# Loading v as rows behind the turn, 64x64 tap tiles and a reordered front in a convolution-plus-MLP kernel

## The chip, the cores and the metric

The kernel runs on one core of one Trainium2 chip. The metric is the device time of one execution in microseconds. The profile names the engines PE (TensorE matmul), PEld (TensorE weight load), DVE (VectorE), ACT (ScalarE), POOL (GpSimd) and SP (SyncE, which issues most DMAs).

## The reference

One sequence of 2048 tokens with 512 channels, all inputs bf16:

```python
x = A_q
# block A, on q = layernorm(x)
k_shift[t] = sum_j k[t - j] * shift_k[:, j]            # 4 taps, each channel by itself
kv = k_shift * v
y  = causal_convolution(kv, ssm_k) + kv * ssm_D        # length 2048, each channel; fft in the reference
h  = x + layernorm(x) * y
# block B
h2 = h + relu(layernorm(h) @ w1) @ w2                  # w1 512x1376, w2 1376x512
```

## The kernel before, in words

The long convolution is computed with a two-stage transform of length 4096 made of matrix products. A token is written as 64a + t, with a from 0 to 31 and t from 0 to 63. Every engine works through its own instructions in the order in which the program issues them (`manual_schedule`): the lists of calls in the code are the schedule.

**Start.** `load_rows` (L96) loads ssm_k as rows into `kfl`: partition 32 rg + a, then t, a half d and 64 channels, in runs of 128 bytes. Two of the four quarters `rg` are issued on SP, two on ACT. SP then issues four pairs of DMA transposes, a chunk of 512 tokens of k into `kT` and of v into `vT` (channels on partitions), then the first 512 tokens of x (`x0`), then w1. POOL, DVE and ACT meanwhile make the tables: index patterns by iota, angles by `_turns` (DVE), sines by `_sin` (ACT): `f1hi` and `f1lo` for the first stage, `tab` for the second. `negated` (POOL, L224) writes the negative copies of `tab`. `wdiag` holds the tap weights as diagonal 128x128 matrices.

**Front.** Eight first-stage blocks of ssm_k (`stage1`, L297), 64 small products each in four tiles of 32 rows, with ssm_D added as a spike at time zero; two evictions per block into `a1k`, one on ACT and one on DVE. Eight `taps` (L335): four diagonal products for each of two channel groups of a 512-token chunk, whose eviction on DVE multiplies by v in place (L342). Sixteen `second_k` (L360): the second stage of ssm_k, in place in `a1k`. Four `row` calls (`to_rows`, L285) turn the product k*v, as pairs of bf16 in 32-bit words, into the row layout `xfl`. Between them stand the statistics and the normalisation of the first 512 tokens (`stats`, `norm_rows`), the column means of w1 (PE, ACT) and its centring (POOL, L378).

**Pairs.** `stage1_pairs` (L320): the first stage of the row data, eight blocks, evicted into `a1x`.

**Product.** For each of 16 `kp`, `product` (L484) makes the second stage of `a1x` in two orders (`u2`, `u1`) and multiplies both by `a1k`: one on DVE, the other on DVE too or, for ten of the sixteen, through a copy on ACT (`usb`) on POOL (L498). `last_table` writes the tables of the inverse's last stage.

**After it** come the inverse transform, the gate with x and its norm, the two MLP products with ReLU on ACT, and the output, in an order written out by hand.

PSUM is eight banks as four tiles of two banks, handed out in turn from two pools (`bank2`, L278). SBUF pools are opened and closed as the work proceeds, and a new pool takes the bytes of a closed one: its first writer waits for the last readers of what lay there.

Of the kernel before, what the change touches and what calls it, by code (L numbers as in the profile page):

```python
# [15 lines left out]
P = 128  # L16
# [39 lines left out]
def kernel(  # L56
# [37 lines left out]
    kfl = front.tile([P, 64, 2, 64], BF16, name="kfl")  # L94

    def load_rows(eng, rg):  # L96
        for d in range(2):
            src = bass.AP(tensor=A_ssm_k.tensor, offset=A_ssm_k.offset + S * (P * rg + 64 * d), ap=[[64, 32], [S, 64], [1, 64]])
            eng.dma_start(out=kfl[32 * rg:32 * rg + 32, :, d, :], in_=src)

    wsh = consts.tile([P, DC, KS], BF16, name="wsh")
    nc.scalar.dma_start(out=wsh[:], in_=A_shift_k.rearrange("(r p) j -> p r j", p=P))
    scratch = rows.tile([P, 4096], I32, tag="r", name="scratch")
    drow = scratch[:, 4064:4096].bitcast(BF16)
    nc.gpsimd.memset(drow, 0.0)
    nc.scalar.dma_start(out=drow[0:P:16, :], in_=A_ssm_D.rearrange("(r g) -> r g", g=64))
    load_rows(nc.scalar, 1)
    for rg in (0, 2):
        load_rows(nc.sync, rg)
    vT = front.tile([P, DC, S], BF16, name="vT")  # L110
    CH = 512
    kT = [front.tile([P, DC, CH + 16], BF16, name=f"kT{c}") for c in range(4)]
    nc.vector.memset(kT[0][:, :, 0:16], 0.0)
    for c in range(4):
        if c == 0:
            nc.sync.dma_start_transpose(out=kT[c][:, :, 16:CH + 16], in_=k_d[0:CH, :])
        else:
            nc.sync.dma_start_transpose(out=kT[c][:], in_=k_d[CH * c - 16:CH * c + CH, :])
        nc.sync.dma_start_transpose(out=vT[:, :, CH * c:CH * c + CH], in_=v_d[CH * c:CH * c + CH, :])

    x0 = front.tile([P, 4, D], BF16, name="x0")
    for b, src in enumerate(_tokens(x_d, 0, 4)):
        nc.sync.dma_start(out=x0[32 * b:32 * b + 32].rearrange("p t d -> p (t d)"), in_=src)


    w1 = w1p.tile([P, DC, DFF], BF16, name="w1")
    for i in range(2):
        for d in range(2):
            nc.sync.dma_start(out=w1[64 * i:64 * i + 64, 2 * d:2 * d + 2],
                                in_=B_w1.rearrange("(c i d g) f -> i d g c f", c=2, i=2, d=2)[i, d])  # L130
# [31 lines left out]
    r2 = scratch[:, 0:1024].rearrange("p (a b) -> p a b", b=64)  # L162
    nc.gpsimd.iota(r2, pattern=[[2, 16], [128, 64]], base=1, channel_multiplier=0)
    ident = consts.tile([P, P], BF16, name="ident")
# [8 lines left out]

    ind = consts.tile([P, P], BF16, name="ind")
    nc.gpsimd.memset(ind[:], 0.0)
    for s in range(0, P, 32):
        nc.gpsimd.affine_select(out=ind[s:s + 32, :], in_=ind[s:s + 32, :], compare_op=ALU.not_equal, fill=1.0,
                                base=0, pattern=[[-1, P]], channel_multiplier=4)

# [11 lines left out]
    load_rows(nc.scalar, 3)  # L191
# [11 lines left out]
    nc.gpsimd.memset(f1w[:], 0.0)  # L203
    for rg in range(DC):
        for i, f in enumerate((f1hi, f1lo)):
            nc.gpsimd.tensor_copy(out=f1w[32 * rg:32 * rg + 32, i, rg % 2, :], in_=f[32 * rg:32 * rg + 32, :])
    wdiag = rows.tile([P, DC, KS, P], BF16, name="wdiag")
    for rg in range(DC):
        nc.gpsimd.tensor_tensor(out=wdiag[:, rg, :, :], in0=ident[:].unsqueeze(1).to_broadcast([P, KS, P]),
                                in1=wsh[:, rg, :].unsqueeze(2).to_broadcast([P, KS, P]), op=ALU.mult)  # L210
    wm = rows.tile([P, 4, 344], F32, name="wm")
    ones = consts.tile([P, P], BF16, name="ones")
    nc.gpsimd.memset(ones[:], 1.0 / D)

    def turns2(i, b):
        ta = scratch[:, 1024 * (b + 1):1024 * (b + 2)].rearrange("p (a b) -> p a b", b=64)
        _turns(ta, r2, n2c[:], 8192, o2[:, i, b:b + 1])
        return ta
# [7 lines left out]

    o2 = consts.tile([P, 2, 2], F32, name="o2")
    for i in range(2):
        for b in range(2):
            nc.vector.tensor_scalar(out=o2[:, i, b:b + 1], in0=n2c[:], scalar1=32.0 * i, scalar2=4096.0 + 2048.0 * b,  # L230
                                    op0=ALU.mult, op1=ALU.add)
    for b in range(2):
        sines2(0, b, turns2(0, b))
    negated(0)
    negated(1)
# [12 lines left out]
    nc.gpsimd.iota(r3[:], pattern=[[1, 64]], base=0, channel_multiplier=0)  # L248
    for i, (top, bottom) in enumerate(((64.0, 96.0), (48.0, 80.0), (32.0, 64.0), (6144.0, 8192.0))):
        nc.gpsimd.memset(ow[0:64, i:i + 1], top)  # L250
        nc.gpsimd.memset(ow[64:128, i:i + 1], bottom)
    for i in range(3):
        nc.gpsimd.tensor_scalar(out=t3[:, i, :], in0=r3[:], scalar1=n2c[:], scalar2=ow[:, i:i + 1], op0=ALU.mult, op1=ALU.add)
    nc.gpsimd.memset(hsc[:], 0.0)
    nc.gpsimd.memset(hbi[:], 0.0)
    nc.gpsimd.tensor_scalar(out=k1o[:], in0=k1c[:], scalar1=2.0, scalar2=1.0, op0=ALU.mult, op1=ALU.add)
    for b in range(4):
        q = slice(32 * b, 32 * b + 32)
        nc.gpsimd.memset(hsc[q, b % 2:b % 2 + 1], TURN / 8192)
        nc.gpsimd.memset(hbi[q, b % 2:b % 2 + 1], -0.5 * TURN)  # L260
        nc.gpsimd.tensor_scalar(out=ofc[q], in0=k1o[q], scalar1=32.0 * (b % 2), scalar2=ow[q, 3:4], op0=ALU.mult, op1=ALU.add)
    nc.gpsimd.iota(rf[:], pattern=[[1, NT], [16, 2], [64, 32]], base=0, channel_multiplier=0)
    nc.gpsimd.tensor_scalar(out=rf[:], in0=rf[:], scalar1=k1o[:], scalar2=ofc[:], op0=ALU.mult, op1=ALU.add)
# [21 lines left out]
    def to_rows(src, q, fl):  # L285
        words = src[:].bitcast(F32).rearrange("p c (a b) -> p c a b", b=32)
        pst = bank2("pst")
        for i in range(8):
            nc.tensor.transpose(out=pst[:, i // 4, P * (i % 4):P * (i % 4) + P], in_=words[:, :, :, 8 * q + i], identity=identw[:])
        nc.vector.tensor_single_scalar(out=fl[:].bitcast(I32)[:, :, :, 8 * q:8 * q + 8],  # L290
                                       in_=pst[:].bitcast(I32).rearrange("p b (i d g) -> p g d (b i)", i=4, d=2),
                                       scalar=0, op=ALU.bitwise_or)
# [4 lines left out]
    def stage1(fl, a_out, gb, engs, spike=False):  # L297
# [9 lines left out]
        for gi in range(8):  # L307
            for f, first in ((f1hi, True), (f1lo, False)):
                for rg in range(4):
                    rw = slice(32 * rg, 32 * rg + 32)  # L310
                    nc.tensor.matmul(out=outs[rg][:, gi, :], lhsT=fl[rw, 8 * gb + gi, :, :].rearrange("p d n -> p (d n)"),  # L311
# [23 lines left out]
    def taps(c, h):  # L335
        ps = bank2("pkv")
        for i in range(2):
            for j in range(KS):
                nc.tensor.matmul(out=ps[:, i, :], lhsT=wdiag[:, 2 * h + i, j, :],  # L339
# [58 lines left out]
    def stats(src, mv, r, q):  # L398
        for i in range(4):
            nc.vector.bn_stats(out=st[:, i, :], in_=src[:, i, :])  # L400
# [359 lines left out]
```

## Time and profile before

| | us |
|---|---|
| median of 3 runs | 211.91 (211.48 to 212.68) |
| the profiled execution | 212.53 |
| its span, first to last instruction | 210.8 |
| granted TensorE clock, mean | 0.984 |
| PE busy | 176.0 (84%) |
| DVE busy | 146.5 (69%) |
| ACT busy | 93.6 (44%) |
| POOL busy | 91.5 (43%) |

The profile is one execution, with times from its span's start. A line of a group reads: source line, engine, operation, output<-inputs, shapes, count | busy us, mean ns of one | idle us just before, and what ended that idle time. A line of the timeline begins with its start and its length in us. A line of stretches gives, after the stretch and its length, the busy time (and number of instructions) of PE, PEld, DVE, ACT and POOL, the granted clock, the DMA share and GB/s.

### The profile page before, as it was taken

The numbers are of one execution on the slowest core, as the hardware profiler recorded it, in microseconds if no ns is written. First come the engines' busy times: TensorE is split into PE (matmuls) and PEld (weight loads), VectorE is DVE, ScalarE is ACT, GpSimd is POOL, SyncE is SP. The second block draws the span as 40 slices with busy tenths as digits, with TensorE's granted clock in tenths as the row PEclk, the third lists the DMA queues.
The fourth block names the chain that finished last, engine by engine and source line by source line (L and its number), as shares of the span: only waits on it lengthen the run. The fifth ranks groups of instructions, "written<-read, shape, count | busy, mean of one in ns | idle before, by whom it ended". The sixth has DMA issues, their size and how long they took to land.

```text
span 210.8 us, 4349 instructions
## 1 busy us (share of the span) xinstructions
PE 176.0 (84%) x1787; PEld 107.3 (51%) x1787; DVE 146.5 (69%) x236; ACT 93.6 (44%) x108; POOL 91.5 (43%) x109
## 2 busy tenths in 40 slices
PE   0329696998989587777796899999999999999993
PEld 0125343557768475665665564545455444444452
DVE  2615988459968689999998987988988381343042
ACT  0333535456288756651399447700560056016400
POOL 4899855402069569999298452031040002002000
PEclk9999997999999999999997999999999999999999
DMA  8999999920000000000780261251250215121012
GB/s 124 217 257 177 161 151 225 218 59 2 3 0 3 3 0 5 0 3 0 193 205 3 50 215 53 50 51 28 69 106 0 60 45 99 25 50 25 3 45 55
DMA packets 47315, 16.00 MB, mean 76 GB/s; under 512 B 42720, under 2 KB 46144, under 8 KB 47296
## 3 DMA queue, kind: packets, MB, share of 16 engines
q1 hardware_dynamic: 38400, 14.61, 35.5%
q10 hardware_dynamic: 8896, 1.12, 3.4%
q8 instruction: 14, 0.23, 0.5%
q14 instruction: 5, 0.04, 0.1%
HBM read 7.54 MB, written 2.10 MB: 46 GB/s over the span
## 4 chain that ended last, share of the span: by engine, by line
PE 59%; DVE 24%; ACT 4%; issue 4%; DMA 3%; ACTq 2%; POOL 1%; DVEq 0%; POOLq 0%
PE m L630 18%; PE m L684 17%; PE pkv L339 7%; DVE a1x L493 6%; DVE zs L523 5%; PE u L352 4%; DMA kfl<-in_A_ssm_k_dram 3%; DVE a1k L498 3%; PE pz L550 3%; PE ps L326 3%; PE ps2k L352 3%; DVE xfl L290 2%; ACT a1x L273 2%; PE pz L560 2%; DVE vT L342 2%
## 5 line engine op out<-in xcount | busy, mean ns | idle before, releaser
L666 ACT ACTIVATE h1T<-m 128x512 bf16<-128x512 f32 (+1 forms) x44 | 25.9, 597 | 43.6 <-PE m L630 43.6
L630 PE MATMUL m<-hT,w 128*128 128x512 bf16 (+1 forms) x176 | 39.0, 379 | 0.2 <-ACT hT L597 0.2
L684 PE MATMUL m<-w,h1T 128*128 128x512 bf16 (+1 forms) x165 | 36.3, 379 | 0.0
L690 DVE SCALAR_TENSOR_TENSOR o<-m,rstd,hp 128x256 bf16<-128x256 f32 x32 | 13.8, 478 | 27.6 <-PE m L684 26.6
L404 POOL TENSOR_SCALAR rstd<-mv 128x4 f32<-128x4 f32 x8 | 1.8, 228 | 71.2 <-DVE mv L402 71.2
L630 PEld LDWEIGHTS <-w 128*128 128x128 bf16 (+1 forms) x176 | 17.4, 100 | 20.4 <-issue 0.8
L498 POOL TENSOR_TENSOR a1k<-usb,a1k 128x1024 fp32r<-128x1024 f32 x10 | 23.7, 2396 | 5.3 <-DVE a1x L493 5.2
L684 PEld LDWEIGHTS <-h1T 128*128 128x128 bf16 (+1 forms) x165 | 15.9, 98 | 19.4 <-issue 0.3
L352 PE MATMUL u<-a1x,tab 64*128 64x256 f32 x256 | 19.8, 292 | 6.5 <-DVE a1x L493 2.4
L531 ACT CAST a1x<-zs 128x1024 fp32r<-128x1024 f32 (+2 forms) x10 | 17.2, 1717 | 11.9 <-DVE zs L523 11.9
L352 PEld LDWEIGHTS u<-a1x,tab 64*128 64x128 f32 x256 | 16.4, 185 | 9.8 <-issue 4.9
L493 DVE TENSOR_TENSOR a1x<-u,a1k 128x1024 fp32r<-128x1024 f32 x16 | 19.1, 1217 | 2.4 <-PE u L352 2.4
L529 POOL CAST a1x<-zs 128x1024 fp32r<-128x1024 f32 (+1 forms) x8 | 15.6, 1955 | 8.3 <-DVE zs L523 8.3
L523 DVE STREAM_TRANSPOSE zs<-pi 128x1024 f32<-128x1024 f32 x16 | 18.4, 1213 | 0.5 <-PE pi L518 0.5
L339 PE MATMUL pkv<-kT,wdiag 128*128 128x512 bf16 x64 | 18.5, 441 | 0.2 <-ACT a1k L273 0.2
L518 PE MATMUL pi<-a1k,wd 128*128 128x512 f32 x32 | 13.9, 434 | 2.9 <-DVE a1k L496 1.1
L342 DVE TENSOR_TENSOR vT<-pkv,vT 128x1024 bf16<-128x1024 f32 x8 | 9.8, 1221 | 9.2 <-PE pkv L339 8.2
L273 ACT CAST a1k<-ps2k 128x1024 fp32r<-128x1024 f32 x12 | 11.7, 1013 | 8.8 <-PE ps2k L352 8.8
L492 ACT COPY usb<-u 128x1024 f32<-128x1024 f32 x10 | 10.1, 1017 | 10.6 <-POOL a1k L498 8.7
L518 PE MATMUL pi<-a1x,wd 128*128 128x512 f32 x32 | 13.1, 408 | 0.0
L275 DVE CAST a1k<-ps 128x1024 fp32r<-128x1024 f32 x8 | 9.6, 1215 | 5.0 <-PE ps L311 5.0
L224 POOL TENSOR_SCALAR tab<-tab 128x1024 fp32r<-128x1024 f32 x4 | 11.0, 2775 | 4.4 <-ACT tab L146 4.3
(104 smaller groups left out, 268.3 us busy)
## 6 DMA issues: line engine op xcount, KB each, us to landing
xall<-in_A_q_dram SPq DMA_DIRECT2D x16, 128.0 KB, 3.3
out_dram<-o SPq DMA_DIRECT2D x62, 32.0 KB, 1.6
w<-in_B_w_dram SPq DMA_DIRECT2D x4, 344.0 KB, 7.3
w<-in_B_w_dram SPq DMA_DIRECT2D x1, 1280.0 KB, 6.2
kfl<-in_A_ssm_k_dram SPq DMA_DIRECT2D x4, 256.0 KB, 5.2
kfl<-in_A_ssm_k_dram ACTq DMA_DIRECT2D x4, 256.0 KB, 6.4
x<-in_A_q_dram SPq DMA_DIRECT2D x4, 128.0 KB, 3.8
hT<-hp SPq DMA_TRANSPOSE x7, 3.2
```

Source lines behind the costliest of these rows:

```text
L273: nc.scalar.copy(out=o, in_=i)
L339: nc.tensor.matmul(out=ps[:, i, :], lhsT=wdiag[:, 2 * h + i, j, :], rhs=kT[c][:, 2 * h + i, 16 - j:CH + 16 - j], start=(j == 0), stop=(j = ...
L352: nc.tensor.matmul(out=ps[:, d, 256 * i:256 * i + 256], lhsT=tab[rw, k1, b:b + 2, :].rearrange("p b k -> p (b k)"), rhs=a_in[rw, c, k1, :] ...
L493: nc.vector.tensor_tensor(out=spot(a1x, kp), in0=u2[:], in1=kk.bitcast(F32), op=ALU.mult)
L498: (nc.gpsimd if pool else nc.vector).tensor_tensor(out=kk, in0=(usb if pool else u1)[:], in1=kk.bitcast(F32), op=ALU.mult)
L518: nc.tensor.matmul(out=ps[:, b, :], lhsT=wd[:, m:m + 2, :].rearrange("p b k -> p (b k)"), rhs=src[:, d, 16 * b:16 * b + 16, c0:c0 + 32], s ...
L523: nc.vector.transpose(out=zs[:], in_=ps[:].rearrange("p b (k c) -> p c (b k)", c=32))
L529: nc.gpsimd.tensor_copy(out=o, in_=i)
L531: nc.scalar.copy(out=o, in_=i)
L630: nc.tensor.matmul(out=ps1[:fsz].rearrange("p (i t) -> p i t", i=4), lhsT=w1[:, c, fc * P:fc * P + fsz], rhs=hT[sc][:, c // 2, :, c % 2, : ...
L666: nc.scalar.activation(out=h1T[:fsz, fc, :], in_=ps1[:fsz], func=ACT.Relu)
L684: nc.tensor.matmul(out=ps2[:], lhsT=lhsT, rhs=w2[:ksz, fc, :], start=(fc == 0), stop=(fc == NFC - 1))
```

## The change

What it does, part by part:

- **Loads.** `kfl` becomes two tiles, one for each half of the 64 values of t, and each is loaded by its own pieces of half the size (first-stage block gb reads tile gb // 4). Three quarters `rg` go on SP and one on ACT. v is no longer transposed: it is loaded like ssm_k, as rows, into `vfl` (two tiles, 16 DMAs on SP, 128-byte runs), behind the four transposes of k. w1 comes behind v, in two DMAs, and x's first 512 tokens last, straight into `qn0`.
- **Channels** are grouped in another order throughout (256 a + 128 d + 64 e instead of 128 r + 64 d); gate and MLP only rename their axes.
- **Taps** use 64x64 diagonal blocks in the four quadrants of the array; the result is copied to `ksh` by ACT or DVE, unmultiplied.
- **Turn.** `to_rows` turns `ksh`, and DVE multiplies by `vfl` while it evicts, in two operations for each row call.
- **Zero products.** `warm(14)` issues 14 products of zeros at the head of TensorE's queue.
- **Order.** Tables and diagonals are made in functions called between the blocks, first-stage blocks, taps and second-stage blocks get a new order and new eviction engines, `second_k(11)` moves into the product. `xfl` gets a pool of its own (`xp`) that opens when `early`, the pool of the small index and angle tiles, closes.
- **First norm.** The norm of the first 512 tokens leaves DVE (before the pairs) and becomes, inside the product, sums, squares and scaling on ACT with accumulated outputs, and four small operations on POOL.

The core of the diff:

```diff
+    kfl = [front.tile([P, 32, 2, 64], BF16, name=f"kfl{h}") for h in range(2)]
+    vfl = [front.tile([P, 32, 2, 64], BF16, name=f"vfl{h}") for h in range(2)]
+    def load_v(eng, h):
+        for rg in range(4):
+            for d in range(2):
+                src = bass.AP(tensor=A_v.tensor, offset=A_v.offset + D * 32 * h + first_channel(rg, d),
+                              ap=[[64 * D, 32], [D, 32], [1, 64]])
+                eng.dma_start(out=vfl[h][32 * rg:32 * rg + 32, :, d, :], in_=src)
+    zero = consts.tile([P, 512], BF16, name="zero")
+    nc.vector.memset(zero[:], 0.0)
+    load_rows(nc.scalar, 1, 0)
...
+    for rg in (0, 2, 3):
+        load_rows(nc.sync, rg, 0)
     nc.scalar.dma_start(out=wsh[:], in_=A_shift_k.rearrange("(r p) j -> p r j", p=P))
+    for rg in (0, 2, 3):
+        load_rows(nc.sync, rg, 1)
...
-        nc.sync.dma_start_transpose(out=vT[:, :, CH * c:CH * c + CH], in_=v_d[CH * c:CH * c + CH, :])
...
+    for c in range(4):
+        load_k(c)
+    load_v(nc.sync, 0)
+    load_v(nc.sync, 1)
+    load_rest()          # w1 in two DMAs, then x into qn0 in four
...
     _sin(f1f[:, 32:64], t1[:, 32:64], 128, neg=True)
-    load_rows(nc.scalar, 3)
+    load_rows(nc.scalar, 1, 1)
...
+    wdiag = rows.tile([P, DC, KS, 64], BF16, name="wdiag")
...
     def to_rows(src, q, fl):
...
-        nc.vector.tensor_single_scalar(out=fl[:].bitcast(I32)[:, :, :, 8 * q:8 * q + 8],
-                                       in_=pst[:].bitcast(I32).rearrange("p b (i d g) -> p g d (b i)", i=4, d=2),
-                                       scalar=0, op=ALU.bitwise_or)
+        vals = pst[:].bitcast(BF16).rearrange("p b (i d g w) -> p d g (b i) w", i=4, d=2, w=2)
+        vv = vfl[q // 2][:, 16 * (q % 2):16 * (q % 2) + 16].rearrange("p (i w) d g -> p d g i w", w=2)
+        for d in range(2):
+            nc.vector.tensor_tensor(out=fl[:, :, d, 16 * q:16 * q + 16].rearrange("p g (i w) -> p g i w", w=2),
+                                    in0=vals[:, d], in1=vv[:, d], op=ALU.mult)
...
-    def taps(c, h):
+    def taps(c, a, eng):
         ps = bank2("pkv")
-        for i in range(2):
-            for j in range(KS):
-                nc.tensor.matmul(out=ps[:, i, :], lhsT=wdiag[:, 2 * h + i, j, :],
-                                 rhs=kT[c][:, 2 * h + i, 16 - j:CH + 16 - j], start=(j == 0), stop=(j == KS - 1))
-        vv = vT[:, 2 * h:2 * h + 2, CH * c:CH * c + CH]
-        nc.vector.tensor_tensor(out=vv, in0=ps[:], in1=vv, op=ALU.mult)
+        for j in range(KS):
+            for e in range(2):
+                for d in range(2):
+                    p = slice(64 * e, 64 * e + 64)
+                    nc.tensor.matmul(out=ps[64 * d:64 * d + 64, e, :], lhsT=wdiag[p, 2 * a + d, j, :],
+                                     rhs=kT[c][p, 2 * a + d, 16 - j:CH + 16 - j], start=(j == 0), stop=(j == KS - 1),
+                                     tile_position=(64 * e, 64 * d), skip_group_check=True)
+        copy(eng, ksh[:, 2 * a:2 * a + 2, CH * c:CH * c + CH], ps[:])
...
+    def norm_sums(i):
+        nc.scalar.activation(out=junk[:], in_=qn0[:, i, :], func=ACT.Copy, accum_out=sums[:, 0, i:i + 1])
+    def norm_means():
+        nc.gpsimd.tensor_single_scalar(out=sums[:, 1, :], in_=sums[:, 0, :], scalar=-1.0 / D, op=ALU.mult)
+    def norm_squares(i):
+        nc.scalar.activation(out=junk[:], in_=qn0[:, i, :], func=ACT.Square, bias=sums[:, 1, i:i + 1], accum_out=sums[:, 2, i:i + 1])
...
+    def pairs_pool():
+        nonlocal xp
+        inverse_tables()
+        pl.pop("early")
+        xp = pl.push("xp", side="right")
...
```

The new order of the front (comments left out; the letters are the eviction engines, A for ACT and D for DVE):

```python
warm(14); s1(2, "AD"); diagonals(); ta01 = turns2(0, 1); sines2(0, 0, ta00)
s1(0, "DA"); sines2(0, 1, ta01); s1(1, "DA"); negated(0); negated(1)
s1(3, "AA"); s1(4, "DA"); s1(6, "AD"); s1(5, "DA"); inverse_turns(); ta10 = turns2(1, 0)
tap(0, "A"); ta11 = turns2(1, 1); sines2(1, 0, ta10); tap(1, "A"); s1(7, "AD"); sines2(1, 1, ta11)
negated(3); negated(2); pair_tables(); tap(2, "D"); tap(3, "A"); second_k(1, "A"); pairs_pool()
tap(4, "A"); second_k(3, "D"); second_k(5, "A"); second_k(4, "D"); tap(5, "A"); tap(6, "D"); tap(7, "A")
second_k(2, "A"); second_k(10, "D"); row(0); second_k(7, "D"); second_k(9, "A"); second_k(0, "A")
second_k(6, "A"); second_k(8, "A"); row(1); second_k(13, "A"); second_k(12, "A"); row(3)
column_means(0); row(2); column_means(1); center(2); center(3)
second_k(15, "A"); second_k(14, "D"); center(0); center(1)      # then the pairs
```

In the product the steps stand behind these kp: `norm_sums` 0 to 3; `last_table(0)` and `norm_means` 4; `last_table(1)` and two `norm_squares` 7; the other two 8; `second_k(11, "A")` and `norm_scales` (three POOL operations) 9; `last_table(2)` 10; `norm_out` (ACT) 11 to 14.

## Prediction

> **What bounds the kernel now.** I read the stages first (busy time by stretch), then the chain that ended last, the timeline at both ends of the front, the costliest groups and the DMA issues. Four stretches: the start to 14.6 us, the front (first stage of ssm_k, taps, second stage, turning) to 61.5, the pairs (first stage of k*v) to 73.1, the product to 101.2. What follows to 210.8 (inverse, gate, MLP) the change only relabels.
>
> ```profile
> core 0: us, PE busy (x) PEld busy (x) DVE busy (x) ACT busy (x) POOL busy (x), PEclk, DMA share, GB/s
> 14.60:61.47 46.87, 41.67 (x777) 26.15 (x778) 34.54 (x41) 22.72 (x25) 22.77 (x41) 0.96 0.69 119
> 61.47:73.13 11.66, 8.76 (x261) 7.61 (x257) 9.52 (x8) 9.60 (x10) 9.73 (x4) 1.00 0.01 3
> 73.13:101.16 28.03, 21.17 (x260) 17.03 (x261) 25.61 (x23) 13.29 (x13) 23.75 (x10) 1.00 0.00 1
> 28.00:34.65 6.65, 5.00 (x216) 2.98 (x214) 6.04 (x7) 3.11 (x4) 2.26 (x4) 0.99 1.23 175
> 34.65:38.20 3.55, 3.55 (x10) 1.11 (x11) 1.29 (x3) 0.91 (x1) 3.55 (x2) 0.54 0.66 160
> ```
>
> TensorE (first column) is busy 41.7 of the front's 46.9 us, ScalarE under half: the front is TensorE's. Pairs are bound by evictions (DVE, ACT), the product by DVE at 25.6 of 28.0 with POOL close behind. The last two rows matter later: after a stretch in which TensorE was 75% busy its clock fell to 0.54.
>
> ```profile
> 7.67 2.37 ACTq L99 DMA_DIRECT2D kfl<-in_A_ssm_k_dram  x1
> ...
> 14.63 0.87 PEld L311 LDWEIGHTS <-kfl 32*128 32x128 bf16 x61 [3.99 <-DMA kfl<-in_A_ssm_k_dram]
> ...
> 16.73 3.57 PE L339 MATMUL pkv<-kT,wdiag 128*128 128x512 bf16 x8
> ...
> 21.21 1.90 PE L339 MATMUL pkv<-kT,wdiag 128*128 128x512 bf16 x8
> ```
>
> In the timeline the first stage begins at 14.63, when the last quarter of ssm_k, issued on ACT at 7.67, has landed. A tap costs 3.57 us on a cold clock, 1.9 (1.84 back to back) on a warm one.
>
> ```profile
> L339 PE MATMUL pkv<-kT,wdiag 128*128 128x512 bf16 x64 | 18.5, 441 | 0.2 <-ACT a1k L273 0.2
> L342 DVE TENSOR_TENSOR vT<-pkv,vT 128x1024 bf16<-128x1024 f32 x8 | 9.8, 1221 | 9.2 <-PE pkv L339 8.2 <-DMA w<-in_B_w_dram 1.0
> L273 ACT CAST a1k<-ps2k 128x1024 fp32r<-128x1024 f32 x12 | 11.7, 1013 | 8.8 <-PE ps2k L352 8.8
> L378 POOL TENSOR_TENSOR w<-w,wm 128x1376 bf16<-128x1376 bf16 x4 | 11.2, 2826 | 1.7 <-ACT wm L374 1.7
> L224 POOL TENSOR_SCALAR tab<-tab 128x1024 fp32r<-128x1024 f32 x4 | 11.0, 2775 | 4.4 <-ACT tab L146 4.3
> L498 POOL TENSOR_TENSOR a1k<-usb,a1k 128x1024 fp32r<-128x1024 f32 x10 | 23.7, 2396 | 5.3 <-DVE a1x L493 5.2
> ```
>
> These are the prices: 18.5 us of taps on TensorE; a 1024-wide eviction 1.0 us on ACT and 1.22 on DVE; 2.78 for a negation, 2.40 for a product multiply and 11.2 for centring w1 on POOL.
>
> **The change, part by part.**
>
> *Start.* The first four first-stage blocks need only half 0 of ssm_k, 1 MB. The first slice of 5.27 us moved 0.65 MB at 124 GB/s, the next ran at 217, so 1 MB is there at 7.1; with a microsecond to land and some of half 1 in between, 8.6. Bounds: f1lo, which the stage also reads, was ready at 7.93; the third quarter of ssm_k landed at 10.55. POOL's affine selects no longer wait 2.2 us for the D row. The gain is 14.63 - 8.6 = 6.0 (4.1 to 6.7). The 14 zero products cost at most 14 x 0.45 = 6.3 us on an idle TensorE from about 1 us on, so nothing.
>
> *Taps.* A tap becomes 16 64x64 products of 512 columns. In the first stage four tiles of 32 rows run together (the timeline has four of L311 in 0.20 us, each 0.19). If four quadrants do likewise, a tap takes 4 x 0.22 = 0.9; if none overlap, 16 x 0.213 = 3.4. I take 0.9, four tiles at once being the nearest row: eight taps 7.2 instead of 14.8 warm. The multiply by v leaves the tap; its eviction is a plain copy, 6 on ACT and 2 on DVE.
>
> *Turning.* Each of four rows now has two bf16 multiplies from PSUM instead of one integer op (L290, 1.21); nearest row L342, 1.22, hence 2.45 each. Bounds: 0.68 (L572, half as wide) and twice 1.22, should the pair-wise stride halve the rate.
>
> *Sums of the front from 8.6.* TensorE: 8 first stages x 0.75 + 7.2 + 15 second stages x 0.61 + 4 rows x 1.05 + means 2.6 = 29.2. ACT: 25 evictions x 1.0 + 4 sines x 1.15 + 2.0 (w3, means) = 31.6. DVE: 14 evictions x 1.22 + 8 row multiplies x 1.22 + three turns x 1.55 + 0.9 = 32.4; the first norm (4.5 us between 48.3 and 54.6) is gone. So the bound leaves TensorE, and ACT and DVE alone would be through at 9.4 + 32.4 = 42.
>
> *POOL makes it later.* The tile xfl, which row(0) writes, now takes the place of the pool "early", whose last reader is the wd scaling on POOL. POOL works in order: negated(0) waits for sines2(0,1), which stands on ACT behind two evictions and a sine, to 13.7; two negations to 19.3; inverse_turns as before 7.7 (21.71 to 29.46), to 27.0; two negations, 32.5; pair_tables 2.3 to 3.9 (3.94 before, under DVE's turns), about 35.6; wd 0.7: 36.3. DVE reaches row(0) at 34.3 and stands there; behind it are queued the eviction of second_k(7) and row(1), and with four PSUM tiles TensorE and ACT soon stand too. From 36.3 on DVE has four rows 9.8, two evictions 2.4 and a hole of 1.7 until TensorE has turned row(1): 50.2.
>
> *DMA.* On SP now: 12 half-size pieces of ssm_k, four transposes of k, 16 pieces of v, two of w1, four of x (before: four, four of k and four of v, four of x, four of w1); ACT issues two more of half 1 ahead of its first eviction, 1.2 us each (2.4 at double size). 2.1 MB of ssm_k until 11.9; four transposes at the 163 GB/s of slices 4 to 6, 3.2 each, to 24.8; v's 2.1 MB at 200 (183, what SP issued ssm_k at, to 217), 10.5, to 35.3; w1 at 218, 6.5; with landing 42.8. column_means(0), at 44.1 in my order, waits for w1 and holds row(2) and the pairs behind it on TensorE: 1.3 us of cover, and beyond that one for one.
>
> *Clock.* TensorE idles from 34.9 to 38.8 in this order. After the 75% stretch the clock was 0.54 for 3.55 us; the same here makes a turn and two second stages late by about 1.6 (0 to 3).
>
> The Trainium skill ("TensorE: Matmul & The Clock Gate", Part 1) says that one idle window of about 3.4 us halves the clock and that a busy one restores it. By that rule the gap costs half of 3.4, 1.7. The 3.55 us row agrees.
>
> *Pairs and product.* Pairs: eight DVE evictions x 1.22 from 50.2 to 60.0, plus the clock's 1.6: the product starts at 61.6 instead of 73.13, -11.5. The centring of w1 (11.2 us on POOL) runs from about 48.5 to 59.7, done before POOL's first multiply; if it slipped, the product would slip with it. In the product ACT gains 12 passes x 0.6 and one eviction, 8 us beside 13.3 of 28: covered. POOL gains four small ops, 0.25 + 1.5 us (L404 0.23, the pow of L405 1.04), and it has 0.2 spare per three products: I take +1.2 (0 to 2).
>
> **Sum.** The profiled execution took 212.5 us, 1.7 of it outside its span of 210.8. 212.5 - 11.5 + 1.2 = 202.2; the runs' median is 0.6 lower than it, so 201.6.
>
> **Rivals.** (1) *No tie-ups*: POOL's small ops run faster beside an idle DVE, the clock holds, the start is 7.9: -2.0 - 1.6 - 0.7 - 1.2 = 196.1. For: copies on POOL ran from 0.23 to 0.77 us; against: the 2.78 negations never varied. 0.16.
>
> (2) *v slow, w1 late*: the ACT-queued quarters of ssm_k, in pieces of 128 bytes like v's, went 256 KB in 2.4 us, 109 GB/s. At that v takes 19.2 instead of 10.5, w1 lands at 51.5, 7.4 after it is needed: 209.0. Against: then transposes shared the engines. 0.11. The Trainium skill ("DMA: Bandwidth & Descriptors", Specifications) wants 512 bytes a piece for line rate; here the 128-byte slices moved 217 GB/s and the transposes 163, so the trace doesn't bear the rule out against the transposes.
>
> (3) *The change doesn't do what it says*: the quadrants run one after the other. 8 x 3.4 = 27.3, TensorE's front 49.3 from 8.6, and rows and pairs follow at 57.9; the product at about 69.5: 212.5 - 3.6 + 1.2 - 0.6 = 209.5. Against: L311's overlap. 0.06.
>
> (4) *Slower: the clock stays at half through front and pairs.* TensorE's load there falls to 29.2 of 41 us, 71%, under the 75% after which it read 0.54. A cold tap costs 1.9 times a warm one, a cold first stage 1.24 against 0.75; at 1.75 the front ends at 8.6 + 51.1 = 59.7, pairs 8 x 1.75 more, 73.7: product 0.6 later than now, 213.5. It decides if the granted clock is under 0.55 from the first stage to the last pair. Against: pairs ran 75% busy at 1.00, and a cold TensorE is saturated, which at 38.2 brought the clock back. 0.07.
>
> **Numbers.** Forecast 201.6 with 0.58 (its own range 198 to 205), the rivals 0.40, no change (gains lost in unnamed waits) 0.02. 197 to 208.5 leaves out the better half of rival 1 and most of 2, 3 and 4. Half a percent, 1.1 us, is what a measurement can tell from none. Faster 0.91, same 0.02, slower 0.07.
>
> **What would show it.** First L311 wait gone by 8 to 9.5; taps of 16 in about 0.9 warm; DVE's first row multiply preceded by a wait on POOL's wd near 36; the means preceded by little or no wait for w1; product starting at 60 to 63 and lasting 28 to 30. Wrong if rows start by 34, if TensorE waits over 2 us for w1, or if the stretch after the product isn't 109 to 111 us long.

## The result, and the profile after

The changed kernel took 214.32 us (median of 18 runs, 212.98 to 215.67), the kernel before 212.59 on the same chip (18 runs, 211.47 to 214.06): a ratio of 1.0088, with a 95% interval of 1.0065 to 1.0111. It is slower by 0.9% where 201.6 us, faster by 5%, was forecast. The profiled execution took 214.23 us, its span is 212.4.

One sentence of the section on the change above was wrong: the two tiles of `kfl` are halves of the 64 channels of a group, not of the 64 values of t (those are v's two tiles). In both kernels a piece of 128 bytes of ssm_k is 64 values of t of one channel; a piece of v is 64 channels of one token. No number hangs on it.

The stages after, as stretches of busy time: from the start of the first stage, the front, the pairs, the product.

```profile
core 0: us, PE busy (x) PEld busy (x) DVE busy (x) ACT busy (x) POOL busy (x), PEclk, DMA share, GB/s
12.05:62.50 50.45, 35.94 (x833) 26.84 (x834) 36.16 (x30) 30.10 (x32) 23.49 (x45) 0.79 0.87 136
62.50:73.23 10.73, 9.00 (x256) 7.67 (x257) 10.41 (x9) 8.05 (x8) 7.99 (x3) 1.00 0.01 3
73.23:103.14 29.91, 22.11 (x268) 17.76 (x269) 25.71 (x23) 22.31 (x34) 25.26 (x14) 1.00 0.01 2
```

The bound left TensorE as forecast: in the front it is busy 35.9 of 50.5 us, no more than DVE, and nobody is busy over 72% of it. But the front is longer than before (50.45 against 46.87), the pairs start at 62.50 instead of the forecast 50.2, and the product lasts 29.9. What follows the product is 109.3 us (212.44 - 103.14; 109.6 before).

The chain of waits at the head of the kernel:

```profile
1.91 5.40 DMA drow<-in_A_ssm_D_dram
...
7.33 4.59 DMA kfl<-in_A_ssm_k_dram
...
12.05 1.05 PE ps L348 x51
```

The first stage still waits for ssm_k, and starts at 12.05, not at 8.6. The costliest groups that answer to the prices of before, then POOL and DVE in the timeline:

```profile
L328 DVE TENSOR_TENSOR xfl<-pst,vfl 128x1024 bf16<-128x1024 bf16 x8 | 14.9, 1927 | 3.2 <-PE pst L324 2.8 <-POOL wd L304 0.4
...
L267 POOL TENSOR_SCALAR tab<-tab 128x1024 fp32r<-128x1024 f32 x4 | 11.2, 2825 | 11.7 <-ACT tab L172 11.7
...
L379 PE MATMUL pkv<-kT,wdiag 64*64 64x512 bf16 x128 | 9.4, 437 | 1.1 <-ACT ksh L308 1.1
```

```profile
34.87 5.72 POOL L267 TENSOR_SCALAR tab<-tab 128x1024 fp32r<-128x1024 f32 x2 [4.68 <-ACT tab L172]
...
42.74 0.69 POOL L304 TENSOR_SCALAR wd<-w 128x192 fp32r<-128x192 f32 x1
```

```profile
43.47 3.75 DVE L328 TENSOR_TENSOR xfl<-pst,vfl 128x1024 bf16<-128x1024 bf16 x2 [0.36 <-POOL wd L304]
47.13 1.22 DVE L310 CAST a1k<-ps2k 128x1024 fp32r<-128x1024 f32 x1
51.17 11.19 DVE L328 TENSOR_TENSOR xfl<-pst,vfl 128x1024 bf16<-128x1024 bf16 x6 [2.82 <-PE pst L324]
```

The taps cost 9.4 us instead of 18.5. POOL stood 4.68 us before its second pair of negations, for ACT's sine. DVE's first row multiply stands behind POOL's `wd`, the place that the prediction named, but at 43.5 instead of 36.3. And a row multiply takes 1.93 us, not 1.22: the last six alone hold DVE for 11 us up to the pairs.

Stage by stage, the profiled execution against the forecast (whose own sum was 202.2):

| | forecast | after | difference |
|---|---|---|---|
| start of the first stage | 8.6 | 12.05 | +3.45 |
| from there to the end of `wd` | 27.7 | 31.4 | +3.7 |
| from there to the pairs | 13.9 | 19.05 | +5.1 |
| pairs | 11.4 | 10.73 | -0.7 |
| product | 29.2 | 29.9 | +0.7 |
| rest | 109.6 | 109.3 | -0.3 |

They add up to +12.0 us, the whole distance from the forecast's sum to the profiled execution (214.23). The experiments look for the cause of each.

### The profile page after: what moved, and what is told of

It reads as the page before. It is cut to its first block, busy times and chain, and to the rows that moved or that the text cites. A ratio compares the mean times of both kernels' runs of the same rounds, so it can differ in the third digit from the quotient of the medians.

```text
span 212.4 us, 4547 instructions
## 1 busy us (share of the span) xinstructions
PE 175.8 (83%) x1861; PEld 110.5 (52%) x1865; DVE 148.4 (70%) x224; ACT 106.3 (50%) x133; POOL 89.6 (42%) x113
## 4 chain that ended last, share of the span: by engine, by line
PE 48%; POOL 16%; DVE 14%; issue 10%; ACT 5%; DMA 5%; POOLq 0%; DVEq 0%
PE m L738 18%; PE m L792 17%; POOL tab L267 5%; DVE zs L631 5%; POOL a1k L591 5%; DVE xfl L328 5%; PE ps L363 3%; PE pz L658 3%; DMA drow<-in_A_ssm_D_dram 3%; DMA kfl<-in_A_ssm_k_dram 2%; PE pz L668 2%; DVE a1x L586 2%; ACT junk L471 1%; PE u L392 1%; PE m L794 1%
## 5 line engine op out<-in xcount | busy, mean ns | idle before, releaser
L774 ACT ACTIVATE h1T<-m 128x512 bf16<-128x512 f32 (+1 forms) x44 | 25.9, 597 | 43.5 <-PE m L738 43.5
L792 PEld LDWEIGHTS <-h1T 128*128 128x128 bf16 (+1 forms) x165 | 16.0, 98 | 19.3 <-issue 0.3
L586 DVE TENSOR_TENSOR a1x<-u,a1k 128x1024 fp32r<-128x1024 f32 x16 | 19.2, 1219 | 4.1 <-PE u L392 3.0
L631 DVE STREAM_TRANSPOSE zs<-pi 128x1024 f32<-128x1024 f32 x16 | 18.5, 1216 | 0.6 <-PE pi L626 0.6
L418 POOL TENSOR_TENSOR w<-w,wm 128x1376 bf16<-128x1376 bf16 x4 | 11.1, 2821 | 15.9 <-ACT wm L414 15.9
L310 DVE CAST a1k<-ps 128x1024 fp32r<-128x1024 f32 x7 | 8.4, 1220 | 13.4 <-PE ps L348 13.4
L328 DVE TENSOR_TENSOR xfl<-pst,vfl 128x1024 bf16<-128x1024 bf16 x8 | 14.9, 1927 | 3.2 <-PE pst L324 2.8
L348 PE MATMUL ps<-f1hi,kfl 32*128 32x64 bf16 x256 | 9.2, 230 | 8.4 <-issue 4.6
L308 ACT CAST a1k<-ps 128x1024 fp32r<-128x1024 f32 x9 | 9.0, 1012 | 12.6 <-PE ps L348 12.6
L308 ACT CAST a1k<-ps2k 128x1024 fp32r<-128x1024 f32 x11 | 10.9, 1021 | 5.6 <-PE ps2k L392 5.6
```

The lines of the kernel that those rows point to most:

```text
L308: nc.scalar.copy(out=o, in_=i)
L328: nc.vector.tensor_tensor(out=fl[:, :, d, 16 * q:16 * q + 16].rearrange("p g (i w) -> p g i w", w=2), in0=vals[:, d], in1=vv[:, d], op=ALU ...
L586: nc.vector.tensor_tensor(out=spot(a1x, kp), in0=u2[:], in1=kk.bitcast(F32), op=ALU.mult)
L631: nc.vector.transpose(out=zs[:], in_=ps[:].rearrange("p b (k c) -> p c (b k)", c=32))
L774: nc.scalar.activation(out=h1T[:fsz, fc, :], in_=ps1[:fsz], func=ACT.Relu)
L792: nc.tensor.matmul(out=ps2[:], lhsT=lhsT, rhs=w2[:ksz, fc, :], start=(fc == 0), stop=(fc == NFC - 1))
```

## The experiments

All ratios are to the kernel before, run on the same chip, with 95% intervals.

### First theories: the queue, the norm, the clock

**The queue.** On SP the 12 pieces of ssm_k took 13.1 us to issue, and the chain names the 1 KB load of D. This kernel puts the D rows first and ssm_k on two queues:

```diff
-    for rg in (0, 2, 3):
-        load_rows(nc.sync, rg, 0)
+    for rg in (1, 3):
+        load_rows(nc.scalar, rg, 0)
+    for rg in (0, 2):
+        load_rows(nc.sync, rg, 0)
```

> The changed kernel with ssm_k's half-0 and half-1 pieces issued as before the change, quarters 0 and 2 on SP and 1 and 3 on ACT, the D row and the tap weights ahead of them on ACT. Theory (loads): the first stage starts at 12.05 because SP's 4th to 6th pieces wait, to 7.33 us, for the landing of DMAs that ACT issued, the last of them the 1 KB D row, and because one queue moves these 128-byte runs at 150 GB/s where two moved 218. Then the first stage starts near 9, everything behind it, POOL's chain too, 3 us sooner, and the run takes 211 to 212 us. Rival (clock): the half clock from 9.8 to 30.3 us sets the front's length; loads sooner bring the first stage forward, but the taps still begin after 26 and the run is within 1 us of the changed kernel, 213.5 to 214.5.

216.71 us, 1.0254 (1.0155 to 1.0354). The first stage started at 11.1, 1 us sooner, and the pairs at 63.5, 1 us later. So another order of issue brought back 1 of the 3.45 us, and none of it reached the pairs.

**The norm's last steps** behind the product's end (`norm_scales` after kp 13, `norm_out` after 15):

> The changed kernel with norm_scales (three POOL operations) behind the last POOL multiply of the product, at kp 13, and the four norm_out behind kp 15. Theory (POOL bounds the product): the 1.6 us of these operations stand between two POOL multiplies and lengthen the product from 28.0 to 29.9; behind them it lasts 28.2 to 28.6 and the run is 1.3 to 1.7 us shorter, 212.6 to 213. Rival (ACT bounds it): ACT's added passes, 22.3 us busy against 13.3, make the copies late; then the product stays at 29.5 to 30 and the run at 214.

214.13 us, 1.0115 (1.0031 to 1.02); the product stayed at 29.91 us. As long as block 11 is in the product too, it costs nothing where those steps stand.

**The clock.** It read 0.5 from 9.8 to 30.3 us after the change. Five zero products ahead of every first-stage block but the first:

```diff
+        if spike and gb != 2:
+            for i in range(5):
+                nc.tensor.matmul(out=pss[0][:, i % 2, :], lhsT=zero[:, 0:P], rhs=zero[:], start=True, stop=True)
```

> The changed kernel with five zero products of 512 columns ahead of each first-stage block but the first, into the block's own PSUM tile, so that TensorE stays busy and keeps its full clock. Rival (clock): the half clock from 9.8 to 30.3 us sets the front's length; the granted clock there rises to 1.00, blocks and taps run at the warm price, the product starts 3 to 5 us sooner and the run takes 209.5 to 211.5. Theory (loads, evictions and POOL's chain set the front): the clock rises, and the run changes by less than 1 us either way, 213.5 to 215.

216.37 us, 1.0191 (1.0077 to 1.0304). The clock averaged 0.85 over the first stage, from 12.64 to 34.36, where the changed kernel had 0.53 from 12.05 to 31.30; the stage ended 3 us later all the same. The zero products took TensorE's time themselves, so this doesn't price the clock; it shows that a warmer clock bought in this way gains nothing.

### Parts of the change, one at a time on the kernel before

Channel halves of ssm_k, on two queues, and nothing else:

> The kernel before with one part of the change alone: ssm_k in channel halves, two tiles, quarters 0 and 2 on SP and 1 and 3 on ACT for both halves. Theory (the front before is TensorE's from the first stage on): the first stage starts at 10 to 11 instead of 14.63 and the whole front moves with it, 3 to 4 us: 208.5 to 209.5. Rival: the next wait is k's transposes or the tables, and the front's end hardly moves: 211.5 to 212.6.

211.14 us, 0.9938 (0.9891 to 0.9985). First stage at 8.6 us (14.63 before): the start that was forecast does exist. Of its 6 us, 2.7 were left at the product's start (70.5 against 73.1): the front from there to the pairs was 50.2 us long instead of 46.9.

The norm in the product, and nothing else:

> The kernel before with one part alone: the first norm on ACT in the product, its POOL operations at kp 4 and 9 as in the change, x loaded straight into qn0. Theory: DVE is freed of 4.5 us between 48.3 and 54.6, where it bound (11.9 of 13.5 us busy), which brings the pairs 3 to 4 us forward; the product becomes 1.5 to 2 us longer by POOL; together 210 to 211. Rival: the pairs wait for something else (second-stage evictions on ACT, w1) and only the longer product shows: 213 to 214.5.

217.4 us, 1.0219 (1.0139 to 1.03). The odd thing stands at the other end of the kernel: the first stage started at 19.2 us instead of 14.63, though ssm_k is loaded as before (only x's first 512 tokens, issued behind the transposes of k and v, go to another tile). Both parts together, the norm's steps late:

> The kernel before with both: channel halves on two queues, and the first norm in the product with its POOL scaling behind kp 13 and its last ACT passes behind kp 15. If the gains of the parts add, 3 to 4 of the start, 3 to 4 of DVE, and nothing lost in the product: 205 to 207. If POOL or ACT still binds the product: 207 to 208.5. If the front has another bound: 210 or more.

214.91 us, 1.008 (1.003 to 1.013), first stage at 11.4 instead of 8.6.

What the norm brings into the first microseconds is a tile: `sums`, 64 bytes a partition. It lies ahead of the tiles of w1, ssm_k, v and k, and moves them all by 64. `kfl` lies at byte 39296 of a partition before, a multiple of 128, and at 40512 after the change, 64 beyond one (`zero` takes 1024 of the 1216 bytes between, `drow` 128, `sums` 64); ssm_k and v arrive in pieces of 128 bytes.

### The place of the tiles

The changed kernel with `sums` twice as long (128 bytes), no other edit:

```diff
-    sums = consts.tile([P, 4, 4], F32, name="sums")
+    sums = consts.tile([P, 8, 4], F32, name="sums")
```

> The changed kernel with one edit: the 64-byte tile sums gets 128 bytes a partition, so that every tile allocated behind it (w1, ssm_k's and v's rows, k's transposes) starts on a multiple of 128 bytes again, as before the change; no instruction differs. Theory (placement): 128-byte runs that straddle a 128-byte line of SBUF move at 150 GB/s, those that don't at 218 or more; the first stage starts at 8.5 to 9.5 instead of 12.05, k and v follow sooner, and the run takes 206 to 210 us. Rival: the number of small DMAs or their queue sets the rate, not the place; then nothing moves, 214 to 214.6.

And the kernel before with an unused tile of 64 bytes:

```diff
+    pad = consts.tile([P, 16], F32, name="pad")
+    nc.gpsimd.memset(pad[:], 0.0)
```

> The kernel before with one edit: an unused tile of 64 bytes a partition behind the constants, which moves w1, ssm_k's rows and k's and v's transposes 64 bytes up; one memset more on POOL. Theory (placement): the loads slow down as in the two kernels with the norm in the product, the first stage starts at 18 to 19.5 instead of 14.63 and the run takes 215.5 to 217.5 us. Rival: no difference, 212 to 213.

The first took 212.07 us, 0.9937 (0.9894 to 0.9979); the second 217.21, 1.0206 (1.0133 to 1.028). Padding moved the first stage from 12.05 to 9.79, the shift moved it from 14.63 to 19.58. The padded kernel still gained less than was expected: its pairs start 3.5 us sooner (59.01), but pairs and product, at clocks of 0.85 and 0.94 in the profiled execution, took 1.5 us longer. TensorE's timeline, padded and shifted:

```profile
9.79 0.18 PE L348 MATMUL ps<-f1hi,kfl 32*128 32x64 bf16 x1 [2.22 <-DMA kfl<-in_A_ssm_k_dram]
...
19.58 0.23 PE L311 MATMUL ps<-f1hi,kfl 32*128 32x64 bf16 x1 [5.06 <-DMA kfl<-in_A_ssm_k_dram]
```

In the page's row of GB/s by fortieths of the span, before:

```profile
GB/s 124 217 257 177 161 151 225 218 59 2 3 0 3 3 0 5 0 3 0 193 205 3 50 215 53 50 51 28 69 106 0 60 45 99 25 50 25 3 45 55
```

and the same kernel with the unused tile:

```profile
GB/s 99 118 158 235 197 174 188 230 155 2 0 3 3 3 0 3 2 3 0 72 234 84 37 93 183 10 73 25 71 118 0 44 52 104 18 55 24 3 43 54
```

The first four slices, ssm_k and the first transposes, go from 124, 217, 257 and 177 to 99, 118, 158 and 235: the same bytes, later. It is shown in both directions that 64 bytes of displacement cost the start 2.3 us in one kernel and 5.0 in the other, and the whole 1.5% (1.0088 against 0.9937) and 2.1%. Why is not shown, nor which of the displaced tiles matter: v's 16 pieces, of the same size, took 14.5 us to issue displaced and 14.7 padded. The Trainium skill ("DMA: Bandwidth & Descriptors", How a descriptor splits into AXI transactions) has reads begin at a multiple of 256 bytes, and a piece that doesn't begin there pay for bytes it doesn't use. Here it is the written side that moved, for which that section gives no price.

Halves and norm on the kernel before, `sums` padded:

> The kernel before with channel halves and the norm in the product (late POOL scaling and last passes), and sums padded to 128 bytes. Theory (placement): the 3.8 us that it lost against halves alone were the loads'; now the first stage starts at 8.5 as with halves alone and DVE is freed besides: 206 to 209 us. Rival: the norm itself cost them, 214 to 215.

210.61 us, 0.9897 (0.9838 to 0.9956), against 1.008 without the padding; first stage at 8.82, product 28.9 us.

### The row multiplies

The padded kernel, which in three rows multiplies other elements of k and v, in other operand orders: row(0) reads v in a run, row(1) v and PSUM in a run, row(3) PSUM alone in a run, row(2) is as it was. The calls run in the order 0, 1, 3, 2.

> The padded kernel with other operands in three of the four row calls, so that k*v is not what the reference computes there: in row(0) v's operand is read in order, in row(3) the PSUM operand is, in row(1) both; row(2) is as it was. They run in the order 0, 1, 3, 2. Four prices of one 1024-wide multiply, 1.93 us each so far. Theory: v's operand, two bytes in every 256, costs the extra 0.7 us: rows 0 and 1 take 1.22, 3 and 2 take 1.9. Rival: the pairs of two bytes read from PSUM cost it: rows 3 and 1 take 1.22, 0 and 2 take 1.9. If the write in runs of 16 costs it, row(1) stays at 1.9 too.

A single run, 207.58 us. DVE's rows in the timeline:

```profile
40.88 1.29 DVE L333 TENSOR_TENSOR xfl<-pst,vfl 128x1024 bf16<-128x1024 bf16 x2 [0.37 <-POOL wd L304]
...
45.23 1.29 DVE L333 TENSOR_TENSOR xfl<-pst,vfl 128x1024 bf16<-128x1024 bf16 x2 [1.93 <-PE pst L324]
47.47 7.45 DVE L333 TENSOR_TENSOR xfl<-pst,vfl 128x1024 bf16<-128x1024 bf16 x4 [0.95 <-PE pst L324]
```

Rows 0 and 1 take 0.69 us a multiply, rows 3 and 2 1.9. PSUM in pairs costs nothing (row 0 as row 1), PSUM in a run gains nothing (row 3 as row 2): the price is v's, whose elements stand 256 bytes apart for the order in which the row is written. The Trainium skill ("Vector Engine (DVE) Microarchitecture Reference", Measured stream behaviour on trn2) gives 1.73 ns a column where one source hops at every element and 1.05 where all run on, for 32-bit words. The trace agrees that an operand that hops pays: here it is 1.92 us for 1024 columns, 1.88 ns each, and 0.67 ns each with v in a run, less than that section's lower figure.

A version that computes everything, with v in runs: the row buffer in the order d, t, channel.

```diff
-            nc.vector.tensor_tensor(out=fl[:, :, d, 16 * q:16 * q + 16].rearrange("p g (i w) -> p g i w", w=2),
+            nc.vector.tensor_tensor(out=fl[:, d, 16 * q:16 * q + 16, :].rearrange("p (i w) g -> p i w g", w=2),
...
-                                     lhsT=fl[rw, 8 * gb + gi, :, :].rearrange("p d n -> p (d n)"),
+                                     lhsT=fl[rw, :, :, 8 * gb + gi].rearrange("p d n -> p (d n)"),
```

> The aligned changed kernel (e5) with one more edit: the row buffer holds d, t, channel instead of channel, d, t, so that the row multiply reads v and writes its result with 64 channels in a run, and the pairs' stage reads its 64x128 weights at 128-byte steps instead of in one run; the result is the full one. Theory 'the stride of v': six or more of the eight multiplies fall from 1.92 to about 0.7-0.8 us as in e8, and the pairs start not at 59.0 but at 51-53, so a median of 204-206 us, if the pairs still take the 11.8 us of e5. Rival 'PSUM in pieces of 2 bytes': the first operand is now read at 4-byte steps, and the multiplies stay at 1.2 or more: pairs at 54-56, 207-209 us. Rival 'the weights pay': the pairs' stage takes 15 us or more, and the gain of the rows is given back there, 209-212 us.

207.7 us, 0.9775 (0.9737 to 0.9812). The pairs started at 52.80 (59.01 in the padded kernel). The costliest groups:

```profile
L363 PE MATMUL ps<-f1w,xfl 64*128 64x128 bf16 x256 | 11.9, 250 | 0.2 <-DVE xfl L328 0.2
L363 PEld LDWEIGHTS <-xfl 64*128 64x128 bf16 x256 | 11.8, 199 | 0.4 <-issue 0.4
...
L328 DVE TENSOR_TENSOR xfl<-pst,vfl 128x1024 bf16<-128x1024 bf16 x8 | 9.3, 1217 | 1.8 <-PE pst L324 1.4 <-DMA vfl<-in_A_v_dram 0.4
```

Both rivals are partly true. The multiply now costs 1.217 us, not 0.69: v and the output run on, and PSUM, read at every second bf16 element, is the operand that is left (no run changes PSUM's step alone). And a weight load whose columns stand 128 bytes apart takes 199 ns (107 in the padded kernel), so the pairs are TensorE's and last 13.3 us instead of 11.8. The rows give 6.2 us, the pairs take back 1.5. But the padded kernel's pairs ran at a clock of 0.85:

```profile
core 0: us, PE busy (x) PEld busy (x) DVE busy (x) ACT busy (x) POOL busy (x), PEclk, DMA share, GB/s
59.01:70.77 11.76, 10.25 (x256) 9.27 (x257) 10.50 (x9) 8.11 (x8) 7.96 (x3) 0.85 0.01 3
```

At 1.00 the changed kernel's took 10.73, with loads of 94 ns; against that the strided weights cost 2.6 us. That the multiply comes out at the 1.22 of the forecast is chance: for another order of operands.

### The product

The padded kernel with `second_k(11)` back ahead of the pairs:

> e5 (channel-major rows) with only the second stage of block 11 moved from the product's step 9 back ahead of the pairs; the norm's steps are where the change puts them. Theory 'block 11 costs in the product what it takes there': the product lasts 29.2-29.6 us instead of 30.4, and the pairs start at most 0.8 later, so the time stays within 0.6 of e5's 212.1. Rival 'the norm alone lengthens it': the product stays at 30.2-30.5, and the time rises by up to 0.8.

212.3 us, 0.9973 (0.9935 to 1.0011), product 29.89 us where the padded kernel's was 30.39: half a microsecond out of the product, most of it back in front and pairs (which start at 59.27 instead of 59.01), no gain. Next, the token-major kernel with block 11 out and the norm's last steps late:

> e9 with the second stage of block 11 back ahead of the pairs and the first norm's scales and outputs behind the product's last evictions. Theory 'the product is filled by both': it lasts 28.0-28.5 us instead of e5's 30.4, and the front is longer by at most 0.8, so 1.2-2.0 us below e9. Rival 'the product's own waits': it lasts 29 or more, as in e7, and the time is within 0.7 us of e9.

208.61 us, 0.9807 (0.9756 to 0.9857): the gain that was expected didn't come. The product fell from 30.39 to 29.42, but the pairs started at 53.87 instead of 52.80, and the two intervals overlap. Then the norm out of the product, in VectorE's list ahead of the pairs:

> e10 with the first norm undone: it runs on VectorE ahead of the pairs, after the last row, and the product holds only its own work and the three last tables. Theory 'the norm's sums and squares on ScalarE lengthen the product': its length falls from e10's 29.4 to the 28.0-28.2 of the kernel before, and the front grows by up to 4.3 (four statistics of 0.68 and four scalings of 0.41 on VectorE), of which the pairs' start shows at most 4: a time of 208-211 us. Rival 'the product lost its 1.4 to something else' (the storage order, the clock): it stays at 29.0-29.5, and the time is 209-212.

Its three timed runs took 221.4 to 223.4 us, 1.0446 (1.0402 to 1.0491), over all that was expected. The profiled execution took 904.75 us, with matmuls of 512 columns at 1706 ns where they take 379 elsewhere, so no stage can be read from it and the cause stays open. Last, the norm left out:

> e10 without the first norm: the q that enters the fuse is left as it was loaded (this part of the computation is left out), so the product holds only its own work and the three last tables, and nothing is added ahead of the pairs. Theory 'the norm's steps on ScalarE lengthen the product': it falls from e10's 29.4 to 28.0-28.2, the length of the kernel before, and the time is 1.2-1.6 under e10's 208.6. Rival 'something else took the 1.4': the product stays at 29.0 or more and the time within 0.6 of e10's. Either way the pairs start at e10's 53.9.

206.84 us, 0.9736 (0.9672 to 0.9799); this version leaves that part of the computation out. The product as a stretch:

```profile
core 0: us, PE busy (x) PEld busy (x) DVE busy (x) ACT busy (x) POOL busy (x), PEclk, DMA share, GB/s
66.42:94.45 28.03, 20.97 (x260) 17.15 (x261) 25.62 (x23) 13.29 (x13) 23.74 (x10) 1.00 0.01 2
```

28.03 us, to the hundredth the product of the kernel before. So at a full clock the norm and block 11 are all that lengthens it. Among profiles whose clock read 1.00 in the product, it is 28.03 without both, 28.92 with the norm and its last steps late (the last kernel below), 29.91 with the norm and block 11 (the changed kernel, and the same with the last steps late). Profiles with 0.93 or 0.94 there (one half-clock stretch of 3.4 us) run some 0.5 longer for like contents: 30.39 with both, 29.89 with block 11 out, 29.42 with the last steps late besides. So the two costs don't simply add: block 11 out alone gives 0.5, and late steps give another 0.5 only once it is out.

### GpSimd's waits

The sines of the table's second half (ACT) and their turns moved ahead of `s1(5)`, on the version with block 11 out and the norm late:

```diff
+    ta10 = turns2(1, 0); sines2(1, 0, ta10); ta11 = turns2(1, 1); sines2(1, 1, ta11)
     s1(5, "DA"); inverse_turns()
-    ta10 = turns2(1, 0)
-    tap(0, "A"); ta11 = turns2(1, 1); sines2(1, 0, ta10); tap(1, "A"); s1(7, "AD"); sines2(1, 1, ta11)
+    tap(0, "A"); tap(1, "A"); s1(7, "AD")
```

> e10 with the sines of the second half of the table moved ahead of two of the first stage's evictions on ScalarE, and their turns and the inverse turns reordered on GpSimd accordingly. Theory 'GpSimd's waits for ScalarE set the rows': the wait of 4-5 us ahead of the negations goes, the inverse table wd ends near 36 instead of 40, the first row starts there, and the pairs start 2-4 us sooner than in e10, 2-4 us off the time. Rival 'v and w1': the second half of v, which is still loaded until 40 or later, takes over, and at most 1 us comes of it. Rival 'TensorE pays': two evictions late hold the first stage's banks and its blocks end 2 us later, nothing gained.

207.66 us, 0.9771 (0.9697 to 0.9845). `wd` ended at 37.43 instead of 40.88, as the theory had it, but the first row started only 1.2 us sooner (39.75) and the pairs 1.4 (52.44): TensorE turns the row's words behind the copy of the last tap, which ended near 38.5 on ACT. In time the two versions' intervals overlap. Then both column means after the last row:

> e11 with both column means after the last row, so that the last row's transposes do not stand behind products that need w1. Theory 'w1's landing near 44.9 holds the rows': VectorE's rows run on without w1, the last multiply ends 1-2 us sooner, and the means' 2.7 us then stand ahead of the pairs on TensorE: the pairs start at 52 or up to 1 us sooner, 206.5-207.7 us. Rival 'v holds them': nothing changes, within 0.4 us of e11's 207.7. Rival 'TensorE pays': the means stand behind the last row with nothing beside them, pairs 1 us later, 208.5.

206.39 us, 0.9708 (0.9686 to 0.973), the fastest version here: 2.9% under the kernel before and 3.8% under the changed one (0.9708 / 1.0088 = 0.962). Its stretches:

```profile
core 0: us, PE busy (x) PEld busy (x) DVE busy (x) ACT busy (x) POOL busy (x), PEclk, DMA share, GB/s
9.47:52.51 43.04, 35.27 (x842) 25.99 (x842) 30.98 (x30) 30.17 (x32) 23.03 (x45) 0.81 0.88 161
52.51:65.86 13.35, 11.99 (x260) 11.88 (x257) 10.79 (x9) 9.27 (x9) 10.28 (x4) 1.00 0.02 4
65.86:94.78 28.92, 21.09 (x261) 17.16 (x261) 25.62 (x23) 18.68 (x29) 24.41 (x13) 1.00 0.01 1
```

The pairs start at 52.51 against 52.44 with the means between the rows, so w1 wasn't what held them. The time fell within the theory's range, but not for its reason: the pairs moved by nothing, the intervals of the two versions overlap, and their profiled executions took 206.34 and 206.52 us. The product is half a microsecond shorter (28.92 against 29.41), with its clock at 1.00.

## Why the prediction was wrong, step by step

- **What bounds the kernel after: right.** The front left TensorE; DVE's rows behind POOL's `wd` set its end. The sum failed in the sizes of what stands on that path.
- **Start, 8.6 us: wrong by 3.45.** The rate of 217 GB/s was measured with tiles that lay on multiples of 128 bytes. The new `sums` tile moved them by 64. With the tile padded the first stage starts at 9.3 to 9.8, within the bounds (7.9 to 10.6), so the place is 2.3 to 2.8 us of it. The rest fits the queues, but no run changes them alone: the two aligned kernels that split ssm_k evenly between SP and ACT started at 8.6 and 8.8, while the padded one has 12 of 16 pieces on SP. The prediction listed every DMA and no address.
- **Taps, 0.9 us warm: right.** Sixteen 64x64 products overlap in the four quadrants. In the fastest version's chain of waits 48 of them take 2.79 us, 0.93 for 16:

```profile
34.35 2.79 PE pkv L379 x48
```

- **Rows, 1.22 us a multiply: the term that was mis-sized most.** Eight took 1.93 and held DVE for 14.9 us instead of 9.8, which is the +5.1 between `wd` and the pairs (the hole before row(1) was 2.8 instead of 1.7, and one eviction of 1.2 fell behind the rows: these two cancel). The nearest row by shape (L342) had the right width, and one operand in PSUM, but both operands in runs. The bound "should the pair-wise stride halve the rate", 2.44, held 1.93 but was put on the wrong operand: PSUM's pairs are free, v's single elements aren't.
- **POOL: DVE's wait for `wd` right, its date 7.1 us late.** The first negations ended at 22.7 instead of 19.3, which is the late start. Then POOL stood 4.68 us at the second pair of negations for `sines2(1, 1)`, a wait that the forecast had at nothing (27.0 to 32.5 without a gap); 0.95 came back in the f1w copies and `wd`. ACT takes that sine behind evictions of first-stage blocks, which came in pieces: TensorE's weight loads stopped inside the blocks for 2.0 and 2.9 us at "issue", waiting for nothing that the profile shows:

```profile
21.44 0.13 PEld L348 LDWEIGHTS <-kfl 32*128 32x128 bf16 x7 [2.01 <-issue]
...
26.82 0.24 PEld L348 LDWEIGHTS <-kfl 32*128 32x128 bf16 x15 [2.88 <-issue]
```

The same stops, 2.0 and 2.6 us, stand in the padded kernel; their cause is open. That the wait for the sine sets `wd`'s date is shown: with the sines moved ahead, `wd` ended 3.45 us sooner, though the pairs gained only 1.4.

- **DMA: v halfway to the second rival, without its effect.** v's 16 pieces took SP 14.5 us, 145 GB/s, where the forecast had 200 and the rival 109 (14.7 us in the padded kernel, so the place isn't its reason):

```profile
27.42 14.48 SPq L114 DMA_DIRECT2D vfl<-in_A_v_dram  x16
```

w1's two loads were issued behind it, at 41.9 and 42.8, and took 7.2 to 9.3 us to land, so w1 was there near 51, close to the rival's 51.5. The column means didn't wait for it, because the rows were later still: they began at 55.1.

- **Clock: wrong in length.** Forecast was one gap of 1.6 us; it read 0.79 over the front, half from 9.8 to 30.3. What that costs wasn't separated; the zero products don't settle it.
- **Pairs: right within 0.7. Product: +1.9 where +1.2 was forecast**, inside the bound of 2.0: 0.9 of it for the norm with its last steps late, 1.0 for block 11 and for where those steps stand. The eviction and the passes on ACT were not "covered" by ACT's idle half.
- **The slower rival** (a cold clock through front and pairs, 213.5; its own terms add up to 213.7) came near in time but not in kind: the pairs ran at 1.00.

With both mis-sized terms removed (padding, v in runs) the median is 207.7 us, 6 over the forecast. In its profiled execution (207.56, 5.4 over the forecast's sum) the first row is 4.5 late (40.8), the rows are 1.9 shorter (12.0 to the pairs), the pairs 1.9 longer (13.3, the strided weights), the product 1.2 longer (30.4) and the rest 0.3 shorter.

## What to carry to other kernels

Check where a change moves the tiles that DMAs write: a new tile of 64 bytes slowed loads that nobody had touched, by more than the change gained elsewhere. The shape alone didn't price a vector instruction here: at 128x1024 bf16 the same multiply took 0.69, 1.22 or 1.92 us by the steps of its operands. Find the row whose operands run in the same way, or take the worse bound. When the bound moves to a chain across engines (ACT's sine, POOL's negation, POOL's scaling, DVE's row), date every link of that chain by the engine that releases it, since its waits, not its busy time, set the end.

## What the runs showed of the hardware that was not expected

- Loads in pieces of 128 bytes into tiles 64 bytes off a multiple of 128: the first stage of the unchanged kernel started 4.95 us later (19.58 against 14.63), and the kernel was 2.1% slower. v's pieces of the same size showed no such cost (14.5 us to issue displaced, 14.7 not).
- One bf16 operand with its elements 256 bytes apart takes a multiply of 1024 columns from 0.69 to 1.92 us. PSUM read in pairs cost nothing; with PSUM read at every second element and all else in runs it took 1.22.
- A load of 64x128 bf16 weights with columns 128 bytes apart took 199 ns, in a run 94 (both at a clock of 1.00).
